# Attention and snake MLP on one core: earlier TensorE warm-up, alpha's load on another queue, later fills and one shorter lag in the tails, last tile in 384 and 128 columns

## Chip, cores, metric

One NeuronCore of a Trainium2 chip. The metric is the time of one execution on the device in microseconds, as the median of several runs.

## The reference, cut to what matters

```python
# attention with cluster routing: B=4, H=8, S=768, D=64, 16 clusters per head
q_assign = argmax(q_n @ c_n); k_assign = argmax(k_n @ c_n)
scores = where(q_assign == k_assign, q @ k.T / sqrt(D), -1e9)
x = softmax(scores) @ v            # as [3072, 512]
# MLP with the snake activation, 512 -> 2048 -> 512
h = x @ w_in
g = h + sin(alpha * h) ** 2 / (alpha + 1e-9)
out = g @ w_out                    # float32
```

## The kernel before

The kernel goes batch by batch: 48 attention steps for the four head pairs of a batch, then the MLP in 16 blocks of hidden columns (f = 0 to 15). The output has six tiles of 128 rows per batch. Two of them (the "own" products, tiles 1 and 0) are accumulated during the MLP, some blocks behind the hidden products; that distance is the lag. What is left of them comes in the tail, after the first scores of the next batch. The other four tiles are "fill": single products placed between the attention steps of the next batch, where TensorE would otherwise stand.

```python
warm = gT[:, 0, 0:640]
nc.vector.memset(warm, 0.0)
...
nc.sync.dma_start(out=a_sb, in_=moe_alpha.rearrange("(f p) -> f p", p=P))
def warmup(n):                        # n matmuls of 512 columns on `warm`
    ...
warmup(5)
...                                   # end of a batch's attention
own = [(1, OB, 3 if b else 4), (0, M0, 5 if b else 7)]
for f in range(NF):
    hidden_mm(f, A[f % 3], 0, KX)     # TensorE: h of block f (cut)
    snake(f, A[f % 3])                # ScalarE and VectorE: row f of gT
    for mt, bk, lag in own:
        if f >= lag:
            out_mm(mt, f - lag, bk)
def tail(fill, b=b, own=own):
    todo = [(f, mt, bk) for mt, bk, lag in own for f in range(NF - lag, NF)]
    todo.sort(key=lambda x: x[0])
    for f, mt, bk in todo:
        out_mm(mt, f, bk)
        if f == NF - 1:
            out_store(b, mt, bk)      # copy to SBUF, store from SyncE
        if fill:
            fill.go(1)
...                                   # the very end
for lo, bk, eng in ((0, M2, "act"), (DM // 2, OB, "dve")):
    for f in range(NF):
        out_mm(5, f, bk, lo, lo + DM // 2)
    out_store(B - 1, 5, bk, eng, lo, lo + DM // 2)
```

Assignment products (`prep_asn`): for a later pair they multiply transposed q and k with the centroids. From pair 6 on their operand T is put together by eight SBUF-to-SBUF moves from SyncE (`T<-Tq`). Pairs 7 and 8 get their products in step 20 of the second batch.

The softmax here doesn't subtract the row's maximum and nothing guards it: scores larger than these inputs give would overflow.

## Time and profile before

| | |
|---|---|
| time | 309.98 us, median of 3 (309.56 to 310.06) |
| profiled span | 308.44 us (that run took 310.34) |
| TensorE | 97% busy, 80% of the chain that ended last |
| ScalarE, VectorE | 77% and 67% busy, 10% and 5% of the chain |

The chain is the path of work that ended last, followed back from the last instruction to what released each step. A line of a timeline gives start (us), length (us), engine, source line, operation, output<-input, shapes, count, and in brackets the idle time before it and what ended that. Buffer numbers are left out, so M stands for M0, M1 or M2.

The prediction shows the lines that carry the argument. Two more, from the page's part on DMA issues (output and input, queue, count, KB each, median us from issue to landing):

```profile
T<-Tq SPq DMA_DIRECT2D x80, 96.0 KB, 2.9
out_dram<-o_sb SPq DMA_DIRECT2D x23, 256.0 KB, 2.1
```

Both kinds are issued by SyncE, one after the other. The DMAs of SyncE and ScalarE take eight completion semaphores in turn (those of GpSimd take eight others), and each DMA waits for the one that had its semaphore eight places before.

### The profile page before, as it was taken

How to read it: one execution, taken by the hardware profiler on the slowest of the kernel's cores; microseconds unless marked ns; L12 is line 12 of the kernel's file. 1: busy time of each engine (PE TensorE's matmuls, PEld its weight loads, DVE VectorE, ACT ScalarE, POOL GpSimd, SP SyncE). 2: the span in 40 equal slices, each digit the busy share in tenths (PEclk: the TensorE clock that was granted, in tenths of full speed). 3: DMA queues.
4: the chain of work that ended last, by engine and by line, in shares of the span. 5: the costliest groups of instructions: out<-in, count | busy, mean ns of one | idle time of the engine just before them, and what ended most of it. 6: DMA issues, size and time to landing. Idle time of an engine off the chain costs nothing.

```text
span 308.4 us, 7196 instructions
## 1 busy us (share of the span) xinstructions
PE 300.7 (97%) x2726; PEld 178.2 (58%) x2726; DVE 206.2 (67%) x369; ACT 238.2 (77%) x323; POOL 139.6 (45%) x231
## 2 busy tenths in 40 slices
PE   8899999999999999999999999999999999999995
PEld 3476776555465656555556656555556666555544
DVE  3786666999766993687897485677874313677721
ACT  5589997976498998777589989687679999687300
POOL 5779988048355199984005189970001090000000
PEclk9999999999999999999999999999999999999999
DMA  7457999989678476981044577420021121100031
GB/s 224 151 168 219 312 255 240 215 182 327 129 188 189 102 154 155 274 331 51 2 117 111 112 183 165 107 85 2 0 74 57 37 46 41 36 0 2 0 136 68
DMA packets 31105, 40.48 MB, mean 131 GB/s; under 512 B 5904, under 2 KB 24928, under 8 KB 31072
## 3 DMA queue, kind: packets, MB, share of 16 engines
q0 software_dynamic: 10240, 21.11, 26.2%
q1 hardware_dynamic: 20592, 18.87, 23.5%
q8 instruction: 21, 0.34, 0.5%
q14 instruction: 12, 0.10, 0.1%
q10 hardware_dynamic: 240, 0.06, 0.1%
HBM read 27.30 MB, written 6.29 MB: 109 GB/s over the span
## 4 chain that ended last, share of the span: by engine, by line
PE 80%; ACT 10%; DVE 5%; DMA 2%; issue 1%; SPq 0%; DVEq 0%; ACTq 0%
PE M L406 18%; PE S L437 16%; PE S L338 11%; ACT pT L344 10%; PE OB L353 9%; PE M L437 7%; PE S L339 5%; PE OB L406 4%; PE M L222 3%; DVE gT L462 3%; PE S L406 2%; DMA QK<-ohT 2%; PE M L144 2%; DVE u_sb L458 1%; PE S L513 1%
## 5 line engine op out<-in xcount | busy, mean ns | idle before, releaser
L344 ACT ACTIVATE pT<-S 128x768 bf16<-128x768 f32 x192 | 142.3, 809 | 15.9 <-PE S L339 14.8
L406 PE MATMUL M<-w_out_bf,gT 128*128 128x512 bf16 (+1 forms) x288 | 89.6, 373 | 0.2 <-DVE gT L462 0.2
L338 PE MATMUL S<-QK 80*128 80x512 bf16 x192 | 72.9, 380 | 1.9 <-DMA QK<-ohT 0.8
L437 PEld LDWEIGHTS <-w_in_bf 128*128 128x128 bf16 x512 | 49.2, 98 | 38.1 <-issue 2.4
L353 PEld LDWEIGHTS <-pT 128*128 128x128 bf16 x1152 | 56.0, 97 | 21.4 <-DVE xs L365 0.5
L437 PE MATMUL S<-xT,w_in_bf 128*128 128x512 bf16 x352 | 66.2, 326 | 0.4 <-DVE gT L462 0.4
L353 PE MATMUL OB<-VX,pT 128*128 128x65 bf16 x1152 | 61.4, 193 | 0.0
L199 POOL TENSOR_SCALAR QK<-T 64x384 bf16<-64x384 f32 x80 | 42.0, 526 | 38.6 <-DMA T<-Tq 33.7
L450 ACT ACTIVATE s_sb<-S,alpha_col 128x768 bf16<-128x768 f32 (+2 forms) x45 | 39.6, 885 | 23.4 <-PE S L437 16.5
L406 PEld LDWEIGHTS <-gT 128*128 128x128 bf16 x400 | 39.0, 98 | 27.7 <-issue 1.7
L462 DVE SCALAR_TENSOR_TENSOR gT<-u_sb,ralpha,S 128x768 bf16<-128x768 bf16 (+2 forms) x45 | 44.6, 994 | 11.0 <-ACT u_sb L455 8.1
L339 PE MATMUL S<-QK 80*128 80x256 bf16 x192 | 51.9, 270 | 0.0
L399 POOL DMA_DIRECT2D xT<-xq x48 | 25.8, 545 | 25.0 <-DVE xq L391 17.2
L364 DVE RECIPROCAL rec<-OB 128x6 f32<-128x6 f32 x32 | 6.2, 194 | 37.7 <-PE OB L353 37.6
L437 PE MATMUL M<-xT,w_in_bf 128*128 128x512 bf16 (+1 forms) x160 | 30.6, 326 | 0.0
L339 PEld LDWEIGHTS <-QK 80*128 80x128 bf16 x192 | 18.8, 98 | 17.1 <-issue 2.2
L458 DVE TENSOR_TENSOR u_sb<-s_sb 128x768 bf16<-128x768 bf16 (+2 forms) x41 | 23.1, 566 | 6.1 <-ACT s_sb L450 6.1
L211 POOL CAST VX<-v 128x768 bf16<-128x768 f32 x16 | 13.8, 861 | 29.1 <-issue 28.1
L450 ACT ACTIVATE s_sb<-M,alpha_col 128x512 bf16<-128x512 f32 (+1 forms) x40 | 20.9, 573 | 6.9 <-PE M L437 6.8
L406 PE MATMUL OB<-w_out_bf,gT 128*128 128x512 bf16 (+1 forms) x80 | 26.2, 358 | 0.0
L462 DVE SCALAR_TENSOR_TENSOR gT<-u_sb,ralpha,M 128x512 bf16<-128x512 bf16 (+1 forms) x40 | 22.8, 611 | 4.6 <-ACT u_sb L455 4.2
L338 PEld LDWEIGHTS <-QK 80*128 80x128 bf16 x192 | 18.6, 97 | 8.9 <-issue 4.4
(86 smaller groups left out, 276.7 us busy)
## 6 DMA issues: line engine op xcount, KB each, us to landing
T<-Tq SPq DMA_DIRECT2D x80, 96.0 KB, 2.9
out_dram<-o_sb SPq DMA_DIRECT2D x23, 256.0 KB, 2.1
v<-in_v_dram POOLq DMA_DIRECT2D x14, 384.0 KB, 5.0
q<-in_q_dram POOLq DMA_DIRECT2D x13, 384.0 KB, 6.9
k<-in_k_dram POOLq DMA_DIRECT2D x13, 384.0 KB, 7.3
w_in_bf<-in_moe_w_in_dram POOLq DMA_DIRECT2D x4, 512.0 KB, 9.6
w_out_bf<-in_moe_w_out_dram POOLq DMA_DIRECT2D x4, 512.0 KB, 11.1
xT<-xq POOLq DMA_DIRECT2D x48, 24.0 KB, 2.2
```

The costliest lines, as they stand in the source:

```text
L199: nc.gpsimd.tensor_scalar(out=QK[0:D, m % NQK, h, t].rearrange("c (n i a) -> c i n a", i=4, a=32)[:, 2 * par : 2 * par + 2], in0=src[:, t] ...
L211: nc.gpsimd.tensor_copy(out=VX[m % NVX][:, :, :, 0:D], in_=st[m]["v32"])
L338: nc.tensor.matmul(out=dst[:, 0:512], lhsT=lhsT, rhs=T[:, 0, 0:512], start=True, stop=True)
L339: nc.tensor.matmul(out=dst[:, 512:S], lhsT=lhsT, rhs=T[:, 0, 512:S], start=True, stop=True)
L344: nc.scalar.activation(out=pT, in_=area(i)[:, 0:S], func=ACTF.Exp, scale=escale)
L353: nc.tensor.matmul(out=o3[:, j, :], lhsT=pT[:, P * j : P * j + P], rhs=VX[m % NVX][:, h, jof(m // NHP, kt), :], start=(kt == 0 and j == 0) ...
L399: nc.gpsimd.dma_start(out=xT[32 * g : 32 * g + 32, 0:2, QS * i : QS * i + QS], in_=xq[0].rearrange("p (h g n) -> p h g n", h=2, g=4)[32 * ...
L406: nc.tensor.matmul(out=bk[:, lo:hi], lhsT=gT[:, f, P * mt : P * mt + P], rhs=w_out_bf[:, f, lo:hi], start=(f == 0), stop=(f == NF - 1),)
L437: nc.tensor.matmul(out=ar[lo // 512][:, 0 : hi - lo] if isinstance(ar, tuple) else ar[:, lo:hi], lhsT=lhsT, rhs=xT[:, kk, :].rearrange("c ...
L450: nc.scalar.activation(out=s_sb[:, lo:hi], in_=src, func=ACTF.Sin, scale=alpha_col[:, f : f + 1])
L458: nc.vector.tensor_tensor(out=u_sb[:, lo:hi], in0=s_sb[:, lo:hi], in1=s_sb[:, lo:hi], op=ALU.mult)
L462: nc.vector.scalar_tensor_tensor(out=gT[:, f, lo:hi], in0=u_sb[:, lo:hi], scalar=ralpha[:, f : f + 1], in1=src, op0=ALU.mult, op1=ALU.add,)
```

## The change

The intent: keep TensorE from standing. Warm it sooner, take a small load off SyncE, do not start fill in the tail while its bank is still read, and shorten what follows the last matmul.

```diff
-    warm = gT[:, 0, 0:640]
-    nc.vector.memset(warm, 0.0)
+    ones = nc.const_aps.tensor(1.0, (P, 512), BF16)
...
-    nc.sync.dma_start(out=a_sb, ...)
+    nc.gpsimd.dma_start(out=a_sb, ...)
...
-                lhsT=warm[:, 0:P], rhs=warm[:, P:640],
+                lhsT=ones[:, 0:P], rhs=ones,
...
-    warmup(5)
+    warmup(6)
...
-        own = [(1, OB, 3 if b else 4), (0, M0, 5 if b else 7)]
+        own = [(1, OB, 3 if b else 4), (0, M0, 5 if b else 6)]
...
-            for f, mt, bk in todo:
+            for n, (f, mt, bk) in enumerate(todo):
...
-                if fill:
-                    fill.go(1)
+                if fill and n > 2:
+                    fill.go(2 if n < 6 else 1)
...
-    for lo, bk, eng in ((0, M2, "act"), (DM // 2, OB, "dve")):
+    for lo, hi, bk, eng in ((0, 384, M2, "act"), (384, DM, OB, "dve")):
         for f in range(NF):
-            out_mm(5, f, bk, lo, lo + DM // 2)
-        out_store(B - 1, 5, bk, eng, lo, lo + DM // 2)
+            out_mm(5, f, bk, lo, hi)
+        out_store(B - 1, 5, bk, eng, lo, hi)
```

More of the change, by code (lines that the diff above doesn't have):

```diff
@@ L508 @@
     load_qk(1)
-    nc.sync.dma_start(out=a_sb, in_=moe_alpha.rearrange("(f p) -> f p", p=P))
+    nc.gpsimd.dma_start(out=a_sb, in_=moe_alpha.rearrange("(f p) -> f p", p=P))
     def warmup(n):
@@ L514, in warmup @@
                 out=SA[1][:, 512:1024],
-                lhsT=warm[:, 0:P],
-                rhs=warm[:, P:640],
+                lhsT=ones[:, 0:P],
+                rhs=ones,
                 start=True,
```

## The prediction

> **What bounds the kernel now.** I first read the page's busy times and slices, then the chain that ended last.
>
> ```profile
> PE 300.7 (97%) x2726; PEld 178.2 (58%) x2726; DVE 206.2 (67%) x369; ACT 238.2 (77%) x323; POOL 139.6 (45%) x231
> PE   8899999999999999999999999999999999999995
> PE 80%; ACT 10%; DVE 5%; DMA 2%; issue 1%; SPq 0%; DVEq 0%; ACTq 0%
> ```
>
> TensorE (PE) carries 80% of the chain, ScalarE (ACT) 10%. Busy time overstates a pipelined engine, so I took the distances from one matmul's start to the next: 215.5 ns for 512 columns, 109 ns for 256, 29 ns for the 65-column products. Time beyond these distances, summed per 10 us, is 4.3 us in the first ten, 3.5 us in the second, 1 to 2 us per ten up to 60 us, and after that 0.3 to 1.7 us, nearly all of it small fp32 assignment products. So from 60 us on TensorE runs without gaps but for a few, and a gain there needs a gap that can be closed or work that can move into one. The change touches three places. The start, on TensorE's timeline:
>
> ```profile
> 1.26 2.31 PE L513 MATMUL S<-gT 128*128 128x512 bf16 x5 [1.26 <-DVE gT L496]
> 3.53 0.87 PE L144 MATMUL M<-ident_f,q 128*128 128x128 f32 x3
> 6.09 0.87 PE L236 MATMUL M<-T,cnB 128*32 128x192 f32 x8
> 6.89 0.33 PE L144 MATMUL S<-ident_f,q 128*128 128x128 f32 x1
> ```
>
> The five warm-up matmuls wait for a memset and run at half speed (starts 427 ns apart). The q transposes start at 3.53, when the first q load has landed (issue 0.74, landing 3.40). The granted clock in this profile becomes full at 6.89. Then the end of the first MLP, the first tail (TensorE, and VectorE beside it):
>
> ```profile
> 78.18 0.38 PE L406 MATMUL M<-w_out_bf,gT 128*128 128x512 bf16 x1
> 78.77 1.24 PE L406 MATMUL M<-w_out_bf,gT 128*128 128x512 bf16 x5 [0.20 <-DVE gT L462]
> 77.97 1.14 DVE L462 SCALAR_TENSOR_TENSOR gT<-u_sb,ralpha,M 128x512 bf16<-128x512 bf16 x2
> ```
>
> The matmul at 78.18 is an own product. The next in order is the first fill product; its bank M1 is still being read by the VectorE instruction that makes gT row 14. Start to start is 0.59 us where 0.2155 would do: 0.37 us are lost. An earlier gap in the same MLP:
>
> ```profile
> 61.42 0.38 PE L406 MATMUL OB<-w_out_bf,gT 128*128 128x512 bf16 x1
> 62.17 1.46 PE L437 MATMUL S<-xT,w_in_bf 128*128 128x512 bf16 x8 [0.37 <-DVE gT L462]
> ```
>
> 0.54 us are lost, again waiting for VectorE. In the second tail there is no such gap: its products run from 149.94 to 153.60 at 215.5 ns each, and so do those of the third. Last, the end:
>
> ```profile
> 301.26 1.91 PE L406 MATMUL M<-w_out_bf,gT 128*128 128x256 bf16 x16
> 303.01 1.91 PE L406 MATMUL OB<-w_out_bf,gT 128*128 128x256 bf16 x16
> 303.25 0.37 ACT L419 COPY o_sb<-M 128x256 f32<-128x256 f32 x1 [8.11 <-PE M L406]
> 304.96 0.42 DVE L417 COPY o_sb<-OB 128x256 f32<-128x256 f32 x1 [2.75 <-PE OB L406]
> ```
>
> The last copy takes 0.42 us, its store 1.70 us from issue (305.41) to landing (307.11), and closing waits fill the rest to 308.44.
>
> **What the Trainium skill says.** "TensorE: Matmul & The Clock Gate", section "What's actually happening": the array starts at half clock and goes to full after a busy window of about 3.4 us; the window runs freely, so the moment varies between runs. The trace agrees on the halves (427 and 215.5 ns); from the first matmul to full clock it shows 5.6 us. The same page, "Back-to-back issue gap": columns over 2.4 plus 2.5 ns when isolated, but about 81 ns for 128 columns in a stream with weight loads. The trace contradicts the stream figure: 65-column products with a fresh 128x128 weight each go at 29 ns, 128-column bf16 transposes at 55. "DMA: Bandwidth & Descriptors", "Issuing engines are not separate DMA queues": another issuing engine only saves issue time. That fits the trace, where packets of several queues share the engines.
>
> **The change, part by part.**
>
> *Warm-up from a constant.* The constant is written by GpSimd before the opening barrier, which releases TensorE at about 0.72, so I put the first matmul at about 0.85 instead of 1.26. Six at 427 ns end at 3.41, inside the wait for q (3.40 plus about 0.1 to start). Hence the transposes start when they did, and the gain can only come through an earlier full clock. If it were full by 3.5, the normalised centroids' transpose would end 0.2 us sooner (0.27 against 0.47 latency), the two warm-ups at 5.10 would save 2 x 0.21, and the assignment matmuls would end near 6.35 instead of 6.96: 0.6 us at most, through the one-hot, its move (landing 11.83) and the first scores (11.96). If the window boundary stays at 6.89: nothing. The start moves by 0.4 us, the slope between those extremes is 0.6 us over 3.4, so 0.07 us on average; a now-busier first window can catch an earlier boundary. I book 0.1.
>
> *alpha on GpSimd's queue.* It removes one issue of 0.5 us from SyncE at 4.09. SyncE then idles until 8.97 waiting for VectorE, and data of 8 KB is nothing beside the q and k loads. GpSimd gets an issue of about 0.7 us (its other issues) at 3.4; its next work, the cast at 5.64, waits for ACT. alpha itself is read at 21.03. Booked: 0.
>
> *Own lag 7 to 6, first MLP only.* One more own product (215.5 ns) runs at f=6, right after the product at 61.42: from 61.64 to 61.85, inside the gap that ends at 62.17. Its bank M0 is free, since the VectorE transpose that read it ended at 60.56. One product leaves the tail, where TensorE has no slack: 0.22 us.
>
> *Fill from the fourth own product on.* The first tail now issues four own products before a fill. Starting at 78.18 the first fill comes at 78.18 + 4 x 0.2155 = 79.04; M1 is free at about 78.72. The own ones need gT rows 10 to 12, done by 77.5. The last own row 15 comes at place 16, at 81.6, against 80.69 for its gT. So the gap of 0.37 goes and none comes. The number of fills in this tail drops from 11 to 10; the missing one is made later, among the ten granted at f=2 of the next MLP (9 were left, now 10), so it costs what it saves. The other two tails only change order; their gaps were nil: 0. From 84 us on TensorE is the bound and no load is issued by an absolute clock, so the 0.59 us should reach the end.
>
> *Last tile in 384 and 128 columns.* Matmuls before: 32 x 109 = 3.49 us; after: 16 x 162 + 16 x 55.5 = 3.48, nothing. The final VectorE copy: 0.69 us for 512 columns and 0.42 for 256 give about 0.285 for 128, which saves 0.135. The store: 256 KB land in 2.0 us and 128 KB in 1.7, so 64 KB in about 1.55, saving 0.15. The other store grows to 192 KB but starts near 304.6 (its matmuls end 304.0, the ACT copy of 384 columns takes about 0.47) and lands near 306.5, before the last at about 306.8. Sum 0.29 us.
>
> Sum: 0.1 + 0.22 + 0.37 + 0.29 = 0.98, so 309.98 - 1.0 = 309.0.
>
> **The rivals.** (1) The first-tail gain is given back: ACT or VectorE becomes the bound and scores wait instead. For it: around 20 to 48 and 227 to 237 us the chain runs through exponentials. Against it: both follow TensorE's earlier work and shift with it; after the tail ACT had idled 3.34 us for scores. It would leave 309.5. (2) The 128-column products are bound by weight loads at the stream figure of 81 ns: 16 x 26 = 0.4 us lost, so the last tile gains nothing: 309.4. The 29 ns speak against. (3) The clock catches the earlier window in every run: 0.6 instead of 0.1, 308.5. The 5.6 us of this profile and the page's free-running window speak against its being regular. (4) The new DMA order costs: semaphores rotate among DMAs, so each later one waits on another predecessor; since all shift by one, the distance stays the same. I expect 0; a collision would cost some tenths.
>
> **Range and chances.** The three runs before span 0.5 us (309.56 to 310.06), which may be the clock window. One rival either way is half a microsecond: 308.4 to 309.6. A change of 2% is 6.2 us; nothing here is near that. Faster 0.01, same 0.98, slower 0.01.
>
> **What would show it.** In the changed profile: first matmul near 0.85 and the q transposes still at 3.5; in the first tail no wait of TensorE for gT, and the second scores about 0.8 us closer to the first (one own and one fill product less plus the gap); one more M0 product filling the wait near 62; equal times in the other tails; the last copy near 0.29 us and its store near 1.55. I am wrong if the time from the first tail to the end grows by more than the one repaid product, if the head gets longer, or if 128-column matmuls start 80 ns apart.

## The result

The changed kernel takes 308.67 us (median of 6, 308.47 to 309.38); the kernel before, with the runs beside it, 310.06 us (median of 6, 309.56 to 311.06). The ratio is 0.9956, 95% interval 0.9939 to 0.9973: some 1.4 us less, "same" at the 2% line but clear of zero. A ratio here is always the mean time of one kernel's runs over that of the other's of the same rounds, so not quite the ratio of the medians quoted.

The profiled run's span is 306.53 us against 308.44. The page of the changed kernel, busy times and chain by engine:

```profile
PE 300.6 (98%) x2727; PEld 177.9 (58%) x2727; DVE 206.6 (67%) x368; ACT 238.3 (78%) x323; POOL 140.4 (46%) x232
PE 86%; ACT 10%; DVE 1%; issue 1%; DMA 1%; SPq 0%; ACTq 0%; DVEq 0%
```

VectorE's share of the chain fell from 5% to 1%. The work is the same, so I compared the same instructions by their start in the two traces:

| mark (us) | before | after | lead |
|---|---|---|---|
| first scores of all | 11.96 | 11.41 | 0.55 |
| first scores of batch 2 (ahead of the first tail) | 77.86 | 77.31 | 0.55 |
| second scores of batch 2 (behind it) | 83.51 | 82.17 | 1.34 |
| first scores of batch 3 | 149.61 | 148.38 | 1.23 |
| last scores | 259.24 | 258.04 | 1.20 |
| issue of the last store | 305.41 | 304.07 | 1.34 |
| its landing | 307.11 | 305.62 | 1.49 |
| SyncE's closing drain (the second of three) | 307.67 | 305.76 | 1.91 |

Four gains: 0.55 at the start, 0.79 in the first tail (of which 0.14 is given back by 259 us), 0.14 plus 0.15 in the last copy and store, and 0.42 behind the landing. The last is not in the prediction. TensorE's timeline at the start of the changed kernel:

```profile
0.78 2.72 PE L512 MATMUL S<-const-bfloat16-1.0 128*128 128x512 bf16 x6 [0.78 <-PEq L816]
3.47 0.87 PE L144 MATMUL M<-ident_f,q 128*128 128x128 f32 x3
6.02 0.66 PE L236 MATMUL M<-T,cnB 128*32 128x192 f32 x8
6.61 0.55 PE L144 MATMUL S<-ident_f,q 128*128 128x128 f32 x3
```

The warm-up starts 0.48 us sooner, the q transposes only 0.06. In this trace the clock is full from 6.33 on (6.89 before), so the assignment products take 0.66 instead of 0.87 us. The first tail, TensorE and then VectorE:

```profile
77.64 0.60 PE L406 MATMUL M<-w_out_bf,gT 128*128 128x512 bf16 x2
78.07 0.38 PE L406 MATMUL OB<-w_out_bf,gT 128*128 128x512 bf16 x1
78.29 0.81 PE L406 MATMUL M<-w_out_bf,gT 128*128 128x512 bf16 x3
78.93 0.38 PE L406 MATMUL OB<-w_out_bf,gT 128*128 128x512 bf16 x1
```

```profile
77.45 1.14 DVE L462 SCALAR_TENSOR_TENSOR gT<-u_sb,ralpha,M 128x512 bf16<-128x512 bf16 x2
```

No bracket with a wait is left. Four own products run at 77.64, 77.85, 78.07 and 78.29; the fill starts at 78.50, after VectorE has left M1. The gap near 61 us:

```profile
61.08 0.38 PE L406 MATMUL M<-w_out_bf,gT 128*128 128x512 bf16 x1
61.62 1.14 PE L437 MATMUL S<-xT,w_in_bf 128*128 128x512 bf16 x6 [0.16 <-DVE gT L462]
```

The added product sits in it; 0.33 us of start-to-start time are still lost. The end:

```profile
300.06 2.76 PE L406 MATMUL M<-w_out_bf,gT 128*128 128x384 bf16 x16
302.66 1.06 PE L406 MATMUL OB<-w_out_bf,gT 128*128 128x128 bf16 x16
302.90 0.48 ACT L419 COPY o_sb<-M 128x384 f32<-128x384 f32 x1 [8.96 <-PE M L406]
303.75 0.29 DVE L417 COPY o_sb<-OB 128x128 f32<-128x128 f32 x1 [2.75 <-PE OB L406]
```

What follows the last store is seen in SyncE's own waits (engine and line, what it waited for, us in total, times, longest) and in the instructions of the closing line (count, durations, first and last start). Before, first waits, then the drain:

```profile
SPq L828 <- DMA out_dram<-o_sb: 1.3, 1, 1.3
```

```profile
L828 SPq DRAIN  x3: 7/7/7, 307.6 to 307.9; - x3
```

After:

```profile
SPq L827 <- DMA out_dram<-o_sb: 0.7, 2, 0.4
```

```profile
L827 SPq DRAIN  x3: 7/7/7, 305.7 to 306.0; - x3
```

SyncE closes the program by waiting for the eight semaphores of these DMAs in a fixed order, about 0.06 us each; three drains follow, and the second of them is the mark used here. Line 828 (827 after) is where the kernel's `TileContext` ends, so these waits are instructions of the program. In the program before, the last store has the semaphore in place 0. SyncE stood 1.3 us at that early wait, until the landing at 307.11, and then still walked through the others: the second drain is 0.57 us behind the landing (0.56 by the rounded marks above). With alpha's load gone from the queues of SyncE and ScalarE every later DMA moved by one place, so the last store has the one in place 7. Now the other waits were over before it landed, and the same drain is 0.14 us behind. This is theory C below.

### The profile page after: what moved, and what is told of

It is laid out like the page before. It is cut to its first block, busy times and chain, and to the rows that moved or that the text cites. A ratio compares the mean times of both kernels' runs of the same rounds, so it can differ in the third digit from the quotient of the medians.

```text
span 306.5 us, 7197 instructions
## 1 busy us (share of the span) xinstructions
PE 300.6 (98%) x2727; PEld 177.9 (58%) x2727; DVE 206.6 (67%) x368; ACT 238.3 (78%) x323; POOL 140.4 (46%) x232
## 4 chain that ended last, share of the span: by engine, by line
PE 86%; ACT 10%; DVE 1%; issue 1%; DMA 1%; SPq 0%; ACTq 0%; DVEq 0%
PE M L406 19%; PE S L437 18%; PE S L338 11%; ACT pT L344 10%; PE OB L353 9%; PE M L437 8%; PE S L339 5%; PE OB L406 5%; PE M L222 3%; PE S L406 2%; PE M L144 2%; PE S L512 1%; DVE gT L462 1%; DMA QK<-ohT 1%; PE OB L377 1%
## 5 line engine op out<-in xcount | busy, mean ns | idle before, releaser
L199 POOL TENSOR_SCALAR QK<-T 64x384 bf16<-64x384 f32 x80 | 42.8, 535 | 39.4 <-DMA T<-Tq 29.0
L458 DVE TENSOR_TENSOR u_sb<-s_sb 128x768 bf16<-128x768 bf16 (+2 forms) x41 | 24.1, 589 | 6.1 <-ACT s_sb L450 6.1
L406 PE MATMUL OB<-w_out_bf,gT 128*128 128x512 bf16 (+1 forms) x80 | 25.3, 347 | 0.0
```

The lines of the kernel that those rows point to most:

```text
L199: nc.gpsimd.tensor_scalar(out=QK[0:D, m % NQK, h, t].rearrange("c (n i a) -> c i n a", i=4, a=32)[:, 2 * par : 2 * par + 2], in0=src[:, t] ...
L406: nc.tensor.matmul(out=bk[:, lo:hi], lhsT=gT[:, f, P * mt : P * mt + P], rhs=w_out_bf[:, f, lo:hi], start=(f == 0), stop=(f == NF - 1),)
L458: nc.vector.tensor_tensor(out=u_sb[:, lo:hi], in0=s_sb[:, lo:hi], in1=s_sb[:, lo:hi], op=ALU.mult)
```

## The experiments

All twelve gave correct results. Each was timed in five rounds beside the kernel before. "Tail" is the distance from the first to the second scores of batch 2, "close" that from the last store's landing to the second of SyncE's closing drains, both from the trace.

| run | median us | ratio to before (95%) | tail | close |
|---|---|---|---|---|
| before, first profile | 309.98 | | 5.66 | 0.57 |
| changed, first runs | 308.67 | 0.9956 (0.9939 to 0.9973) | 4.86 | 0.14 |
| e1 alpha only | 309.57 | 0.9983 (0.9969 to 0.9997) | 5.66 | 0.14 |
| e2 lag only | 309.61 | 0.9993 (0.9974 to 1.0013) | 5.23 | 0.57 |
| e3 fill only | 309.74 | 0.9988 (0.9973 to 1.0003) | 5.29 | 0.57 |
| e4 last tile only | 309.97 | 1.0004 (0.9980 to 1.0029) | 5.66 | 0.57 |
| e5 seven added loads | 309.47 | 0.9977 (0.9965 to 0.9989) | 5.65 | 0.14 |
| e6 warm-up only | 309.83 | 0.9996 (0.9983 to 1.0010) | 5.69 | 0.57 |
| e7 changed, alpha on SyncE | 309.30 | 0.9978 (0.9958 to 0.9998) | 4.86 | 0.57 |
| e8 changed, OB lag 3 | 308.91 | 0.9964 (0.9949 to 0.9979) | 4.43 | 0.14 |
| e9 changed, again | 308.65 | 0.9979 (0.9949 to 1.0009) | 4.86 | 0.14 |
| e10 changed, step 22 | 308.63 | 0.9960 (0.9948 to 0.9972) | 4.86 | 0.14 |
| e11 e10 with the old warm-up | 308.58 | 0.9964 (0.9951 to 0.9977) | 4.86 | 0.14 |
| e12 e10 with OB lag 3 | 308.47 | 0.9955 (0.9943 to 0.9967) | 4.43 | 0.14 |

e1 to e4 ran on one chip, e5 to e8 on a second, e9 to e12 on a third. The intervals are mostly as wide as the effects, so each part is judged by its place in the trace and the time is taken as a check.

**e1, alpha's load alone.**

```diff
-    nc.sync.dma_start(out=a_sb, ...)
+    nc.gpsimd.dma_start(out=a_sb, ...)
```

> Only alpha's load moves from SyncE to GpSimd. Theory C (closing waits): SyncE ends the program by waiting for the eight semaphores of the hardware DMAs in a fixed order; without alpha's load every later DMA moves down one place, so the last store falls from place 0, waited for early, to place 7, waited for last. Expected: last store's landing to SyncE's closing drain 0.14 us instead of 0.56, time down by about 0.4 us (309.6), first scores still at 12.0. Rival H (the freed issue helps the start): first scores up to 0.3 us earlier and nothing at the end. My prediction said 0.

The close falls to 0.14 us, and the time is down by 0.5 us (0.9983), clear of zero. The first scores come at 11.53, which is within what other profiles of the old start show (11.28 to 11.96), so rival H has nothing to show here. From the first scores to the issue of the last store it is 293.50 us, against 293.45 before: the new order of the DMAs cost nothing on the way.

**e5, the same effect without moving alpha.**

```diff
+    pad = const.tile([NF, 7, 8], F32, name="pad")
+    for i in range(7):
+        nc.sync.dma_start(out=pad[:, i], in_=moe_alpha.rearrange("(f p) -> f p", p=P)[:, 0:8])
     spare = [SA[0][:, 0:512], M1, SA[0][:, 512:1024], M2]
```

> The kernel before, alpha still on SyncE, with seven added loads of 512 bytes from SyncE in its idle time some microseconds before the last stores; they only turn the places of the eight semaphores so that the last store gets place 7. Theory C (place of the last store among the closing waits): landing to closing drain 0.14 us instead of 0.56, time down 0.4 us although seven DMAs were added. Rival (it is the queue that alpha is on, or the number of DMAs): no change, or up.

Seven useless loads make the kernel faster: 0.9977, some 0.7 us with an interval from 0.3 to 1.1. SyncE's closing drains in e5:

```profile
L831 SPq DRAIN  x3: 7/7/7, 306.8 to 307.1; - x3
```

Its last store landed at 306.67, 0.14 us before the second of them (306.81). alpha is still on SyncE, so neither its queue nor a smaller number of DMAs is the cause. The place of the last store is.

**e7, alpha back on SyncE in the changed kernel.**

```diff
-    nc.gpsimd.dma_start(out=a_sb, ...)
+    nc.sync.dma_start(out=a_sb, ...)
```

> The changed kernel with alpha back on SyncE. Theory C: landing to closing drain 0.56 again, so 0.4 us slower than the changed kernel (309.1); first scores as in the changed kernel up to the clock's play. Rival H: first scores 0.3 us later, the end unchanged.

```profile
L827 SPq DRAIN  x3: 7/7/7, 308.0 to 308.3; - x3
```

The store landed at 307.50 and the close is 0.57 us again, as theory C wants. The first scores are earlier, not later (10.93), against rival H: the clock was full at 3.58 in this run. Its median of 309.3 is near the 309.1 expected (the changed kernel itself did not run on this chip), but the profiled run is the slowest of six (308.64 to 310.73), for a reason that I had not thought of. TensorE's timeline in it, and its waits in that stretch:

```profile
96.77 0.85 PE L222 MATMUL M<-T,cnB 128*32 128x384 f32 x8
99.49 0.85 PE L222 MATMUL M<-T,cnB 128*32 128x384 f32 x8 [1.86 <-DMA T<-Tq]
```

```profile
PE M L222 <- DMA T<-Tq: 1.9, 1, 1.9
```

The products of pairs 7 and 8 should follow each other by 0.66 us. Those of pair 8 waited for the eight moves that make its T. These were issued from 87.89 and landed by 99.40. The trace's view of the tile, in the stretch of these moves:

```profile
DMA to landing us min/median/max: 5.4/6.2/6.9
```

In the changed kernel's trace they took 4.7 to 5.7 us. SyncE's timeline there, and then in e7:

```profile
87.13 5.20 SPq L176 DMA_DIRECT2D T<-Tq  x8
```

```profile
87.89 5.26 SPq L176 DMA_DIRECT2D T<-Tq  x8
```

In both traces two loads of v from GpSimd, of 384 KB each, are in flight beside the moves: issued at 87.0 and 89.0 and landed by 94.4 in the changed kernel, issued at 87.3 and 89.2 and landed by 96.1 in e7. Between 96 and 98 us the DMA engines are 50% busy in the one and still 89% in the other.

This gave theory D: the change brings TensorE to the product sooner, but not the moves. From the kernel before to the changed one the product of pair 8 came 1.34 us sooner (99.03 to 97.69), the first issue of its moves only 0.14 us (87.27 to 87.13), and the last landing was 0.16 us later (96.95 to 97.11). Between 70 and 97 us SyncE waited 4.2 us for DMAs and 0.3 us for VectorE; no wait for TensorE is listed. The margin is the time at which the products of pair 8 would start, less the last landing. It was 2.07 us in the first profile before, 1.33 to 3.29 in e1 to e5, 0.57 in the changed kernel, 0.19 in e8, -0.14 in e6, and -1.97 here. The landing itself moved between 95.2 and 99.4 us over these profiles.

**e2 and e3, the lag alone and the fill order alone.**

```diff
-        own = [(1, OB, 3 if b else 4), (0, M0, 5 if b else 7)]
+        own = [(1, OB, 3 if b else 4), (0, M0, 5 if b else 6)]
```

> Only the own lag of M0 in the first MLP, 7 to 6. Theory: the product goes into the gap near 62 us, the stall at the first fill of the first tail stays (0.37 us), so the distance from the first to the second scores of the second batch falls from 5.65 to about 5.22 (one own and one fill product fewer), of which one product is paid back later: time down 0.22. Rival: the product has no free gap and the first scores of that batch come 0.2 us later, time unchanged.

TensorE's timeline of e2 keeps the stall:

```profile
77.60 0.38 PE L406 MATMUL M<-w_out_bf,gT 128*128 128x512 bf16 x1
78.19 0.81 PE L406 MATMUL M<-w_out_bf,gT 128*128 128x512 bf16 x3 [0.20 <-DVE gT L462]
```

```diff
-            for f, mt, bk in todo:
+            for n, (f, mt, bk) in enumerate(todo):
...
-                if fill:
-                    fill.go(1)
+                if fill and n > 2:
+                    fill.go(2 if n < 6 else 1)
```

> Only the order of the fills in the tails. Theory: the stall of 0.37 us in the first tail goes and the other two tails do not change (distance of first to second scores 5.65 to 5.28 in the first, 3.99 in the other two): time down 0.37. Rival: the wait moves to own products that now come sooner (gT rows not ready), time unchanged.

That of e3 has none:

```profile
77.64 0.81 PE L406 MATMUL M<-w_out_bf,gT 128*128 128x512 bf16 x3
78.29 0.38 PE L406 MATMUL OB<-w_out_bf,gT 128*128 128x512 bf16 x1
```

The tails, 5.23 and 5.29 us, are those expected (5.22 and 5.28). The other two tails are 4.00 us in every profile, so they did not change. The times are down by 0.2 and 0.4 us, as expected in size, but both intervals hold zero.

**e4, the last tile alone.**

```diff
-    for lo, bk, eng in ((0, M2, "act"), (DM // 2, OB, "dve")):
+    for lo, hi, bk, eng in ((0, 384, M2, "act"), (384, DM, OB, "dve")):
```

> Only the last tile in 384 and 128 columns. Theory: last matmul ends at the same time, the last copy 0.29 instead of 0.42, its store 1.55 instead of 1.70 us, the closing waits still 0.56 us after it because the number of DMAs is unchanged: time down 0.29. Rival: 128-column matmuls go at 80 ns for their weight loads, last matmul 0.4 us later, time up by 0.1.

The end is as predicted: last store 1.55 us from issue to landing, close 0.57. The time shows nothing (1.0004, interval of 0.25% either way). Two of six runs took 310.84 and 311.70, against at most 310.73 for eleven of the kernel before. Its profile has a wait of TensorE for the same kind of move, in the third batch, of 0.36 us:

```profile
178.49 0.85 PE L222 MATMUL M<-T,cnB 128*32 128x384 f32 x8 [0.36 <-DMA T<-Tq]
```

So late moves cost a kernel now and then even where the change did not bring TensorE forward. What happened in the two slow runs is not traced. The run of 311.70 has a mean granted clock of 0.994 on record; all others on record but one (in e9) have 0.998 or more, so lost clock is a rival there.

**e6, the warm-up alone.**

```diff
-    warm = gT[:, 0, 0:640]
-    nc.vector.memset(warm, 0.0)
+    ones = nc.const_aps.tensor(1.0, (P, 512), BF16)
...
-    warmup(5)
+    warmup(6)
```

> Only the warm-up from the constant, six matmuls. Theory: first matmul at 0.78, q transposes still at 3.5, gain only if the clock turns full sooner, on average 0.1 us, between 0 and 0.6 in single runs, so the interval may well hold zero. Rival W (the early start fixes the moment of full clock): first scores at 11.4 to 11.7 in the profile and a clear 0.3 to 0.5 us in the mean.

First matmul at 0.78, q transposes at 3.51, first scores at 11.37, clock full at 6.26. The time is 0.9996: no clear 0.3 to 0.5 us, so rival W has no support, but the interval (0.5 us less to 0.3 us more) does not exclude it, and the kernel also waited for pair 8's moves in its profile (margin -0.14). It is inconclusive about a gain of 0.1 too.

**e8, one more own product moved ahead.**

```diff
-        own = [(1, OB, 3 if b else 4), (0, M0, 5 if b else 6)]
+        own = [(1, OB, 3), (0, M0, 5 if b else 6)]
```

> The changed kernel with one more own product of the first MLP moved ahead (OB lag 4 to 3). After the change TensorE still loses 0.33 us at the same place near 61 us, so one product of 0.2155 us should fit: distance of first to second scores in the first tail 4.86 to 4.43, of which one product is paid back: 0.2 us faster than the changed kernel (308.4). Rival: the product at f=3 finds bank OB still read and pushes the MLP, no gain.

The tail is 4.43 us as expected, and TensorE waits nowhere in its profile between 55 and 80 us. Yet the median is 308.91, not 308.4: three runs lie at 308.36 to 308.60, three at 309.21 to 309.93. The margin for pair 8's moves is down to 0.19 in the profile. Theory D would have it so; e9 to e12 test it.

**e9 and e10, the changed kernel again, and with the assignment product two steps later.**

```diff
-        (7, 1, 20, (25, 26, 31)),
+        (7, 1, 22, (26, 27, 31)),
```

> The changed kernel once more, unchanged, beside the next three on the same chip. Theory D (late transfer): in the second batch the assignment product of pair 8 needs eight SBUF moves that SyncE issues late; TensorE now reaches it 1.5 us sooner, so in some runs it waits (margin 2.07 us in the profile before, 0.57 in the changed one, -1.97 in the profile of the kernel with alpha back on SyncE). Expected 308.6, with one or two runs of six above 309.

> The changed kernel with that assignment product two attention steps later (step 22 instead of 20), nothing else. Theory D: the margin grows by about 1.4 us, no wait of TensorE for the moves in the profile, the slow runs among the fast-state ones disappear (all within 0.5 us), mean 0.1 to 0.3 us under the changed kernel. Rival (the scatter is the clock's moment at the start): scatter and mean unchanged.

The 1.5 us in the expectation is the fall of the margin; TensorE reaches the product 1.34 us sooner. The edit moves the products of both pairs 7 and 8. The changed kernel scatters from 308.38 to 309.06 with one run at 311.81, which alone widens its interval; so two of six are above 309, as expected. With step 22 the five runs lie within 0.42 us (308.38 to 308.80). The margin in the profiles is 2.69 us against 1.29. TensorE's timeline of e10 has all sixteen products in one row:

```profile
98.58 1.50 PE L222 MATMUL M<-T,cnB 128*32 128x384 f32 x16
```

The medians are equal (308.65 and 308.63); what goes is the upper tail, so step 22 is worth nothing in a typical run. The expected gain in the mean, 0.1 to 0.3 us, cannot be told from one outlier. All this fits theory D, but the run of 311.81 has no trace, and five runs against six cannot prove that such runs are gone. A rival stays untested: that run's mean granted clock is 0.994, like that of the run of 311.70 in e4 and of no other, so it may have lost clock, with or without late moves.

**e11, the warm-up judged without the late moves.** The edit is that of e6 undone, on top of e10.

> As the one before, but with the old warm-up (memset, five matmuls). With the late transfer out of the way the difference of these two is the warm-up alone. Theory: first scores at 11.4 to 12.0 with the old one and 10.9 to 11.4 with the new, about 0.3 us in the mean (the four profiles with the new warm-up against six with the old give 11.20 against 11.52); my prediction booked 0.1. Rival: no difference above 0.1.

Mean 308.69 with the old warm-up, 308.58 with the new, a difference of 0.11 us with intervals of about 0.4 us each: the rival ("not above 0.1") cannot be told from a small gain, and the 0.3 us that I expected from the profiles did not show. First scores were at 11.28 and 11.34. Over all fourteen profiles, the seven with the old start have the clock full at 5.22 to 6.89 us (mean 5.81) and first scores at 11.49 in the mean; the seven with the new one 3.58 to 6.33 (mean 5.71) and 11.25. The means differ by 0.1 us where single traces differ by up to 2.75, so no effect of the 0.48 us of earlier start on the clock is shown.

**e12, both additions.** Step 22 and OB lag 3 on the changed kernel.

> Changed kernel with step 22 and OB lag 3 together: the first tail's second scores come 4.43 us after the first, one product is paid back, margin for the moves still about 1.4 us. Theory: 0.2 us under the changed kernel with step 22, the lowest of all, about 308.2. Rival: the lag gains nothing beyond the noise of 0.2.

Mean 308.42 against 308.58 for e10, lowest run 308.09. The size is near the 0.2 expected and the tail is 4.43 us (margin of the moves 1.25), but the intervals overlap: the lowest of all measured, not shown to be faster than the changed kernel.

## Why the prediction was right, and where not

- **Time.** 309.0 predicted, 308.67 measured, inside 308.4 to 309.6. The ratio says 1.36 us less; I had 0.98. That it came so near although a term of 0.43 us was missing is in part luck.
- **Where TensorE stands.** The sums of lost time per 10 us don't come out again exactly: with the same distances, and the whole time of the fp32 products counted, they are 0 to 1.7 us from 60 us on, not 0.3 to 1.7. The reading holds.
- **First tail, 0.37 + 0.22.** Right in place and size. I expected the second scores 0.8 us closer to the first: 5.66 less 4.86, 0.80 (0.79 by the leads). e2 and e3 give the two terms apart, 0.43 (of which one product is repaid) and 0.37. One product is repaid later: the lead falls from 1.34 to 1.20 by the last scores, 0.14 where I had 0.22. Rival 1 (the gain is given back) did not come: 0.65 of the 0.79 us gained here is left then.
- **Last tile, 0.29.** Right term by term: copy 0.291 us (predicted 0.285), store 1.55 (1.55), 162 and 55.5 ns between the products' starts. The rival of 81 ns per 128-column product is dead.
- **alpha, 0.** Wrong, and this is the missing term. The step that failed is in the fourth rival: "since all shift by one, the distance stays the same". That holds between two DMAs. It does not hold for the closing waits, whose order is fixed: there a shift by one took the last store from the first place to the last, and the close from 0.57 to 0.14 us, a gain of 0.43. e1, e5 and e7 show it. The rival looked at the right place, the order of the DMAs, but expected nothing or a loss. In the prediction the "closing waits" between 307.11 and 308.44 were taken as a constant and not looked into; the trace before had them one by one.
- **Warm-up, 0.1.** The mechanism is right (the q transposes stay at their landing, only the clock can gain), and the first profiles' lead of 0.55 us at the start was mostly their luck: the clock of the kernel before became full at 6.89, the latest of all fourteen. Rival 3 (an early clock in every run) did not come: with the new warm-up it was full anywhere between 3.58 and 6.33. e11's difference of 0.11 us agrees with the 0.1 that I booked, and with none.
- **"No load is issued by an absolute clock."** Only half right. The moves of pair 8 hang on SyncE's backlog, not on TensorE, so the lead can turn into a wait. The prediction has no rival in which a transfer becomes the bound, and I did not look for the transfer with the least margin. In the changed kernel's own profile it did not bind (0.57 us left).

The measured terms add up: 0.59 in the first tail by the working of the prediction (0.65 by the leads 0.79 less 0.14), 0.29 at the last store and 0.42 at the close give 1.30 to 1.36 us, against 1.36 by the ratio. That leaves nothing or 0.1 for the start. But the ratio's interval runs from 0.8 to 1.9 us, so the sum is a check and not a proof; what fixes the terms is their place in the traces.

What stays open: how often the late moves cost something in each kernel (only profiled runs show it), why the same eight moves are issued between 85.9 and 88.7 us and land up to 4 us apart (the traces show only that they share the DMA engines with the loads of v), what part lost clock has in the slowest runs, and whether the new warm-up gains anything.

## What to carry to other kernels

Follow the chain beyond the last matmul: copy, store, landing, and the program's closing waits one by one, because one DMA more or less on the queues of SyncE and ScalarE, even at the very start as here, can change which semaphore the last store holds. When TensorE is brought forward, list the transfers that do not come forward with it and work out their margin. With effects of a few tenths of a microsecond, compare marks inside two traces, and let a control that does nothing else, like the seven added loads, decide the cause.

## What the Trainium skill lacked or had wrong

- No page that I used speaks of the closing waits: eight DMA semaphores waited for in a fixed order, about 0.06 us each, so that the place of the last store decides 0.43 us (0.57 against 0.14 from landing to the second drain, in fourteen profiles without exception). It belongs to "DMA: Bandwidth & Descriptors".
- "TensorE: Matmul & The Clock Gate", section "Back-to-back issue gap": about 81 ns per 128-column matmul in a stream with weight loads. Here, with a new 128x128 weight each, sixteen such matmuls go at 55 to 56 ns, 384 columns at 162 to 163, 512 at 215.5, which is the page's "isolated" formula.
- The same page, section "What's actually happening": full clock after some 3.4 us of sustained work, with a free-running window. In fourteen profiles it took 2.8 to 5.6 us from the first matmul, in one of them (e7) less than the page's window. A start 0.48 us sooner made it 0.1 us sooner in the mean, well inside the scatter.
- "DMA: Bandwidth & Descriptors", section "Anatomy of one DMA — SWDGE (gpsimd) path", gives about 2.0 us plus bytes over 436e3 per us for a DMA that GpSimd issues; for one of 96 KB that makes 2.2 us, an estimate from the page. No such fit was found there for DMAs that SyncE issues. Here SyncE's moves of 96 KB take 2.2 to 3.1 us (median 2.3) in the group issued from 96.1 us in the changed kernel, but 5.4 to 6.9 us in the group that came late in e7, beside the loads of v.
